# Tokens of the eight late groups turned by 32x32 blocks on VectorE, the blocks placed by the store

## The chip, the core and the metric

The kernel runs on one core of a Trainium2 chip. The engines of the core are TensorE (PE in the profile, with PEld for its weight loads), VectorE (DVE), ScalarE (ACT), GpSimd (POOL) and SyncE (SP, which issues most of the transfers). The metric is the device time of one execution in microseconds. Shown with the time before are three executions; their median is 906.98 us.

## The reference

Two blocks follow each other. The first is a linear attention with decay over 4 batches, 8 heads, 768 tokens and 64 features a head. The second takes its output as 4 x 768 tokens of 512 features and does a Fourier mix, a normalisation and a two-layer MLP:

```python
X = np.fft.fft(x, axis=1)
X = np.fft.fft(X, axis=2)
u = x + np.real(X).astype(np.float32)
mu = np.mean(u, axis=-1, keepdims=True)
var = np.mean((u - mu) ** 2, axis=-1, keepdims=True)
un = (u - mu) / np.sqrt(var + 1e-06)
ch = np.maximum(un @ w_ch1, 0.0) @ w_ch2
return (u + ch).astype(np.float32)
```

Here w_ch1 is 512 x 2048, w_ch2 is 2048 x 512, and all values are float32.

## The kernel before

Each batch goes through `attn` (six chunks of 128 tokens, `attn_chunk`) and then through `fft_ln`. In `fft_ln` the tokens and features are folded on VectorE, five products with a table give the transform along the sequence (L440, copied to `ys`), and then three passes (t = 1, 2, 0) do the transform along the features: `width` makes five products (L453 to L458) into a PSUM tile `ps`, ScalarE copies parts of it to `bs` and `ds`, and VectorE adds the result to two token tiles of 128 x 512, `u` and `v_` (L509 to L513). These two tiles are a pair, and the pair is a group (b, g) of 256 tokens. Behind t = 0 a single row is handled apart (L519 to L522).

`norm(g)` takes the pair: statistics per token (L470, L471), the inverse deviation `rs` on GpSimd (L474, L475), and for each of the two tiles the normalised tokens `un` on VectorE (L482, two halves of 256 features, the second one reversed). The MLP needs features on the partitions, so TensorE transposes `un` in four 128 x 128 pieces into PSUM (L486), and ScalarE copies them into `ut` (L487). `un` has one buffer.

There are twelve groups, in the order (1, 2, 0) for each batch. The first four (`PLAIN`, all of batch 0 and group 1 of batch 1) keep `ut` on the chip and go through `mlp`: 64 products with w1 (L545, relu by ScalarE and VectorE into `hr`), then 32 with w2 (L559), then `y` (L565, L566) and a store. The last eight (`LATE`: groups 2 and 0 of batch 1, and all of batches 2 and 3) store `ut` to device memory as `utd` (L494), 512 KB a group, and the tokens as `ud` (L497). They are read back when attention and Fourier mix are through: `load_u` (L611) loads two groups as `ur`, and `late(j)` does the MLP of both at once by sums and differences of blocks (L627 and L674 are its products). `combine_weights` prepares the sums of weight blocks for it on VectorE (L604), and L617 to L620 those of the tokens.

Program order comes from `weave`, which mixes generators by estimated durations: batches 1 to 3 are the leading work, and the early groups' `mlp` is drawn in between so that TensorE has something to do. The framework then orders the instructions of each engine anew when the kernel is built, so what stands in a queue is read from the compiled order. Within an engine's queue instructions start in that order, and one that waits holds up all behind it. This holds for SP too: the loads of `k`, `q` and `v` for attention, the stores of `utd` and `ud`, and the loads of `ur` share its queue.

## Time and profile before

| What | Value |
|---|---|
| median of three executions | 906.98 us (904.29 to 907.66) |
| the profiled execution: time, span | 908.43 us, 906.4 us |
| granted TensorE clock, mean of that execution | 0.975 |
| attention of batch 0, weights loaded and rebuilt | up to about 115 us |
| other batches, early groups' MLP in between | up to 513 us |
| late groups' MLP | 513 us to the end |
| transposes at L486 | 96 (24 tiles of four), 118 to 491 us |
| copies at L487 | 24, 13.6 us of ScalarE |
| stores of `utd` | 8, 512 KB each, 3.3 us to landing |

The span is what the trace covers; the time also holds what lies around it. Rows of the trace give the start in microseconds, the duration, engine, line, and output from inputs; in square brackets the engine's idle time just before and what ended it. Rows of the chain that ended last give start, duration, engine, output and line. Rows of waits give who waited for whom, the total, how often, and the longest. Rows of stretches give the stretch and its length, busy time and count for PE, PEld, DVE, ACT and POOL, then granted clock, DMA share and GB/s. Rows of transfers give count, KB each, and median microseconds from issue to landing.

### The profile page before, as it was taken

To read this page: it belongs to the slowest core of one execution; us is meant where nothing else is said; L and a number is where in the kernel's file an instruction comes from. 1 tells how busy PE (TensorE), PEld (TensorE's weight loads), DVE (VectorE), ACT (ScalarE), POOL (GpSimd) and SP (SyncE) were. 2 spreads that over 40 slices of the span, in tenths; PEclk is the share of its full clock that TensorE was granted. 3 is DMA by queue.
4 is the path that set the end of the run, shared out by engine and by line. 5 is a ranking of instruction groups with operands and counts; after the bars stand their busy time and mean duration, and the time that the engine had idled before them with its cause. 6 is when DMAs were issued, how large, how long until landed. Compare 5 with 4: busy or idle time off the path is not lost.

```text
span 906.4 us, 11761 instructions
## 1 busy us (share of the span) xinstructions
PE 826.5 (91%) x4660; PEld 652.9 (72%) x4660; DVE 437.0 (48%) x1006; ACT 209.0 (23%) x467; POOL 90.7 (10%) x108
## 2 busy tenths in 40 slices
PE   4775678699999999999999899999999999999997
PEld 2564566545865578567874588888888888888886
DVE  4779869854532135443567756115531454135410
ACT  3665436620211212223221021002200120012100
POOL 2214211100010110012200100000000000000000
PEclk9988789899999999999999999999999999999999
DMA  9899316611013241344216001110011100110010
GB/s 230 232 249 252 111 52 179 209 39 35 24 47 93 74 120 47 116 141 129 88 47 215 29 1 47 46 35 12 1 59 47 35 1 1 47 47 1 0 35 24
DMA packets 96190, 72.43 MB, mean 80 GB/s; under 512 B 77536, under 2 KB 79080, under 8 KB 96136
## 3 DMA queue, kind: packets, MB, share of 16 engines
q1 hardware_dynamic: 90176, 57.51, 22.3%
q0 software_dynamic: 2496, 7.87, 2.7%
q10 hardware_dynamic: 3464, 6.30, 2.0%
q8 instruction: 37, 0.61, 0.3%
q14 instruction: 17, 0.14, 0.0%
HBM read 50.68 MB, written 20.99 MB: 79 GB/s over the span
## 4 chain that ended last, share of the span: by engine, by line
PE 51%; DVE 5%; issue 1%; DMA 1%; POOL 1%; ACT 0%; POOLq 0%; DVEq 0%; ACTq 0%
PE p L627 21%; PE p L674 21%; PE pm L545 1%; PE pm L559 1%; PE pa L440 1%; PE pa L486 1%; PE pa L290 1%; PE pa L322 1%; DVE stt L470 1%; DVE w1s L604 1%; DVE w2s L604 1%; PE pa L318 1%; POOL rs L475 0%; DVE x L512 0%; DVE x L513 0%
## 5 line engine op out<-in xcount | busy, mean ns | idle before, releaser
L545 PE MATMUL pm<-ut,w 128*128 128x256 f32 x512 | 124.2, 392 | 10.0 <-ACT hr L553 8.2
L559 PE MATMUL pm<-w,hr 128*128 128x512 f32 x256 | 120.6, 602 | 0.0
L545 PEld LDWEIGHTS pm<-ut,w 128*128 128x128 f32 x512 | 95.9, 194 | 26.3 <-ACT hr L553 8.9
L627 PE MATMUL p<-ur,w 128*128 128x256 f32 x384 | 95.1, 382 | 3.3 <-DVE ur L620 1.9
L627 PEld LDWEIGHTS p<-ur,w 128*128 128x128 f32 x384 | 73.3, 191 | 14.5 <-issue 2.3
L559 PEld LDWEIGHTS pm<-w,hr 128*128 128x128 f32 x256 | 44.8, 190 | 40.3 <-issue 38.8
L627 PE MATMUL p<-us,w1s 128*128 128x256 f32 x256 | 66.6, 383 | 0.0
L674 PE MATMUL p<-w,hs 128*128 128x256 f32 x256 | 58.0, 379 | 0.5 <-DVE y L695 0.5
L674 PE MATMUL p<-w2s,hs 128*128 128x256 f32 x256 | 57.9, 379 | 0.0
L674 PE MATMUL p<-w,ha 128*128 128x256 f32 x256 | 57.9, 379 | 0.0
L535 POOL DMA_INDIRECT out_dram<-y,ix x12 | 13.3, 1109 | 409.9 <-DVE y L698 370.9
L627 PEld LDWEIGHTS p<-us,w1s 128*128 128x128 f32 x256 | 49.2, 192 | 6.9
L674 PEld LDWEIGHTS p<-w,hs 128*128 128x128 f32 x256 | 48.5, 190 | 7.5 <-DVE y L695 0.9
L674 PEld LDWEIGHTS p<-w2s,hs 128*128 128x128 f32 x256 | 48.6, 190 | 6.6
L674 PEld LDWEIGHTS p<-w,ha 128*128 128x128 f32 x256 | 48.6, 190 | 6.6
L290 PEld LDWEIGHTS pa<-qT,kT 64*128 64x128 f32 x384 | 30.1, 193 | 25.9 <-ACT qT L279 14.4
L654 ACT COPY ha<-p 128x256 f32<-128x256 f32 x32 | 11.9, 372 | 155.6 <-PE p L627 155.5
L290 PE MATMUL pa<-qT,kT 64*128 64x128 f32 x384 | 36.2, 291 | 11.7 <-ACT qT L279 10.0
L294 DVE TENSOR_TENSOR sc<-pa,decay 128x512 f32<-128x512 f32 x48 | 31.8, 684 | 29.1 <-PE pa L290 26.3
L322 PE MATMUL pa<-sc,v 128*64 128x128 f32 x384 | 31.2, 290 | 9.8 <-DVE sc L294 9.8
L665 DVE TENSOR_TENSOR ha<-p,ha 128x256 f32<-128x256 f32 x32 | 13.6, 425 | 47.1 <-ACT ha L664 47.1
L322 PEld LDWEIGHTS pa<-sc,v 128*64 128x64 f32 x384 | 23.4, 143 | 17.5 <-DVE sc L294 13.4
(141 smaller groups left out, 1188.3 us busy)
## 6 DMA issues: line engine op xcount, KB each, us to landing
raw<-in_moe_w_ch_dram SPq DMA_DIRECT2D x32, 512.0 KB, 5.2
k<-in_k_dram SPq DMA_DIRECT2D x24, 256.0 KB, 3.8
q<-in_q_dram SPq DMA_DIRECT2D x24, 256.0 KB, 3.9
v<-in_v_dram SPq DMA_DIRECT2D x24, 256.0 KB, 3.2
ud<-x SPq DMA_DIRECT2D x16, 256.0 KB, 2.1
utd<-ut SPq DMA_DIRECT2D x8, 512.0 KB, 3.3
u<-ud SPq DMA_DIRECT2D x16, 256.0 KB, 2.6
ur<-utd SPq DMA_DIRECT2D x8, 512.0 KB, 5.6
```

Of the source, the lines that this page charges most:

```text
L290: mm(pss[hi][:, hp, :], lhsT=kT[HD[hi], hp, :], rhs=qT[HD[hi], hp, :], start=True, stop=True)
L294: nc.vector.tensor_tensor(t, pss[hi], decay[:, hi::2, :], op=ALU.mult)
L318: mm(po[HD[hi], hp, :], lhsT=s_old[HD[hi], hp, :], rhs=qs[HD[hi], hp, :], start=(hp == 0), stop=False, skip_group_check=True)
L322: mm(po[HD[hi], hp, :], lhsT=vt[:, 2 * hp + hi, :], rhs=sc[hi][:, hp, :], start=(c == 0 and hp == 0), stop=(hp == HP - 1), skip_group_chec ...
L535: nc.gpsimd.indirect_dma_start(out=out.rearrange("b s d -> (b s) d"), out_offset=row_of(2 + HC * (b + 1) + T - HC), in_=y[:, :], in_offset ...
L545: nc.tensor.matmul(ps, lhsT=w1[:, c, 128 * fc:128 * fc + 128], rhs=ut[:, c, :], start=(c == 0), stop=(c == KO - 1))
L559: nc.tensor.matmul(ps, lhsT=hr[fc // 4][:, fc % 4, 128 * i:128 * i + 128], rhs=w2[:, fc, :], start=(fc == 0), stop=(fc == FO - 1))
L604: V.tensor_tensor(o[:, i:i + n // 2], x[:, i:i + n // 2], y[:, i:i + n // 2], op=op)
L627: nc.tensor.matmul(ps, lhsT=s2.A[a][:, kt, 128 * i:128 * i + 128], rhs=U[b][:, kt, :], start=(first and kt == 0), stop=(kt == 1), skip_gro ...
L654: nc.scalar.copy(a11, two(X))
L665: V.tensor_tensor(a22, two(Z), a22, op=ADD)
L674: nc.tensor.matmul(ps, lhsT=h[a][:, s, i, :], rhs=s2.B[b][:, i, :], start=(first and i == 0), stop=(i == HF - 1), skip_group_check=True)
```

## The change

For the eight late groups, `un` is no longer transposed by TensorE. VectorE transposes each 32 x 32 block of `un` in place of its own position (one instruction for a 128 x 512 tile) into a new tile `uq`, which has one buffer. That leaves 16 blocks of features for each of four bands of 32 tokens on the wrong partitions. Four stores for each tile, one for each band of 32 partitions, put the blocks where `utd` has them, in runs of 32 values (128 bytes). The PSUM tile, the copy to `ut` and the one store of `ut` for each group are gone for these groups. The four early groups stay as they were. From this place on, lines of the new kernel are numbered ten higher at the most (L486 is L492, L611 is L621, and so on).

```diff
-            ut = new(up, [128, KO, G * 128], "ut")
+            plain = (b, g) in PLAIN
+            if plain:
+                ut = uts[b, g] = new(up, [128, KO, G * 128], "ut")
+            else:
+                to = utd[b, g] = dram.tile([128, KO, G * 128], F32, name=f"utd{b}{g}")
             for i in range(G):
...
-                pt = psum_a([128, KO, 128])
-                for c in range(KO):
-                    nc.tensor.transpose(pt[:, c, :], un[:, 128 * c:128 * c + 128], ident)
-                nc.scalar.copy(ut[:, :, 128 * i:128 * i + 128], pt)
+                if plain:
+                    pt = psum_a([128, KO, 128])
+                    for c in range(KO):
+                        nc.tensor.transpose(pt[:, c, :], un[:, 128 * c:128 * c + 128], ident)
+                    nc.scalar.copy(ut[:, :, 128 * i:128 * i + 128], pt)
+                else:
+                    uq = new(np_, [128, DM], "uq", bufs=1)
+                    nc.vector.transpose(uq, un)
+                    for r in range(0, 128, 32):
+                        dst = to[:, :, 128 * i + r:128 * i + r + 32].rearrange("(a d) c n -> d c a n", d=32)
+                        src = uq[r:r + 32].rearrange("p (c a n) -> p c a n", c=KO, n=32)
+                        nc.sync.dma_start(dst, src)
                 yield 0.7
-            if (b, g) in PLAIN:
-                uts[b, g] = ut
+            if plain:
                 return
-            utd[b, g] = dram.tile([128, KO, G * 128], F32, name=f"utd{b}{g}")
-            nc.sync.dma_start(utd[b, g], ut)
             for T in TT[g]:
```

## The prediction

> **What bounds the kernel now.** I read the page's engine table first, then the granted clock and busy time by stage, then the chain that ended last.
>
> ```profile
> PE 826.5 (91%) x4660; PEld 652.9 (72%) x4660; DVE 437.0 (48%) x1006; ACT 209.0 (23%) x467; POOL 90.7 (10%) x108
> 225.00:513.00 288.00, 276.37 (x1693) 192.21 (x1692) 134.52 (x288) 59.52 (x147) 37.07 (x48) 0.99 0.30 91
> 513.00:906.00 393.00, 387.15 (x1784) 339.87 (x1784) 142.81 (x390) 47.69 (x127) 7.68 (x8) 1.00 0.08 26
> ```
>
> From 225 us on TensorE (PE) is busy 96% of the time at a granted clock of 0.99 or 1.00, VectorE (DVE) less than half. The later stage, from 513 us, has no instruction that the change touches. So the question lies between 225 and 513 us: how much PE work and PE idleness goes there, and what replaces it. The chain at one of the eight late groups (batch 2, group 1) reads: start, duration, engine, output, line.
>
> ```profile
> 371.49 0.60 DVE x L513
> 372.10 1.20 DVE stt L470 x2
> 373.91 0.74 POOL rs L475
> 374.67 0.42 DVE un L482
> 375.14 0.76 PE pa L486 x4
> 375.90 0.86 PE pm L559 x2
> 376.76 0.44 PE pa L486 x4
> 378.09 0.24 PE pa L458 x2
> ```
>
> The transposes (L486) stand in PE's queue ahead of the next pair's width products (L453 to L458, ending at 378.33), so PE and the chain both pass through normalisation before the next pair starts. The end of the stage:
>
> ```profile
> 507.69 1.03 PE L627 MATMUL p<-ur,w 128*128 128x256 f32 x4
> 510.16 1.10 PE L627 MATMUL p<-ur,w 128*128 128x256 f32 x4 [1.45 <-DVE y L566]
> 513.14 1.22 PE L627 MATMUL p<-ur,w 128*128 128x256 f32 x2 [1.87 <-DVE ur L620]
> ...
> 505.62 0.33 DVE y L566
> 505.95 2.11 DVE w L604 x2
> ...
> 509.28 0.41 DVE y L565
> 509.69 0.33 DVE y L566
> 510.02 1.13 DVE w L604
> 511.15 0.61 DVE us L617
> 512.48 0.61 DVE ur L620
> ```
>
> Here PE has finished the early groups' products and waits 1.45 + 1.87 = 3.3 us for DVE, which is still combining weights.
>
> **The change, part by part.** It removes 16 sets of four transposes and their 16 ScalarE copies, adds 16 DVE block transposes, and replaces 8 stores by 64.
>
> *Transposes.* A set that follows other work takes 0.44 us (the row at 376.76): 16 x 0.44 = **7.0 us** of PE, all in a stretch where PE is 96% busy. PE also waits for `un` ahead of the first set of a group:
>
> ```profile
> PE pa L486 <- DVE un L482: 4.4, 8, 0.8
> 237.95 0.67 PE L486 MATMUL pa<-ident,un 128*128 128x128 f32 x4 [0.67 <-DVE un L482]
> ```
>
> Of these 4.4 us (225 to 516 us), 0.67 belong to an early group that stays. So **3.7 us** of waiting go too. The ScalarE copies cost nothing now, since no PE wait in that view names `ut`; I count them at nothing in both directions, and without them PSUM buffers only come free sooner.
>
> *What is late next.* The compiled order changes more than the diff. Before, on PE, in batch 2 (`pm` from `w`,`hr` are early-group products used as filler; `pa` from `dt`,`ys` are width products):
>
> ```order
> L486 MATMUL pa_2666<-ident,un_2663 128x128 x4
> L559 MATMUL pm_3205<-w_148,hr_2904 128x512
> L486 MATMUL pa_2675<-ident,un_2672 128x128 x4
> L453 MATMUL pa_2687<-dt,ys_151 128x128
> L454 MATMUL pa_2687<-dt,ys_149 128x129
> ```
>
> After, at the same place on PE:
>
> ```order
> L458 MATMUL pa_2629<-dt,ys_152 128x128
> L453 MATMUL pa_2681<-dt,ys_151 128x128
> L454 MATMUL pa_2681<-dt,ys_149 128x129
> L455 MATMUL pa_2681<-dt,ys_153 128x129
> L456 MATMUL pa_2681<-dt,ys_150 128x128
> L458 MATMUL pa_2681<-dt,ys_152 128x128
> L453 MATMUL pa_2741<-dt,ys_151 128x128
> ```
>
> The three pairs' width products now run back to back, and the next batch's first attention chunk follows at once. Its score products `sc` stand on DVE behind the normalisation of the first two pairs. The costs of the filler and of a chunk, from the chain:
>
> ```profile
> 405.85 1.09 PE pa L290 x16
> ...
> 411.96 1.72 PE pm L559 x4
> 413.68 1.09 PE pa L290 x16
> 414.77 0.61 PE pa L305 x16
> ...
> 419.37 0.44 PE pa L277 x4
> 419.80 1.73 PE pm L545 x8
> ```
>
> An L545 product (two instructions) costs 1.73 / 4 = 0.43 us, an L559 product 0.86 us; a chunk takes 413.68 - 405.85 = 7.8 us. Until the first use of `sc`, PE has width products 1.13 (377.20 to 378.33) twice, 0.7 for the single row, 0.88 for two chunk transposes, 2 + 9 L545 products (4.7), 1.09 and 0.61: about 10.2 us. DVE has, from the same starting point, 0.6 us until its inputs are there, six 128x256 pieces for `ds` (6 x 0.33), four 128x512 pieces for `x` (2.4), two pairs of statistics (2 x 1.2), 0.2, the wait for `rs` less what fills it (374.67 - 373.30 - 0.67 = 0.7), two `un` (2 x 0.67), one block transpose and one `sc` (1.2): about 10.8. PE waits some 0.6 us there and as much for the second `sc`; I take 2 us each time with hand-overs, at two batch changes: **+4 us**.
>
> *The block transpose.* The trace has none. From below, 0.33 us, a 128x256 piece; from above 1.13 us, a 128x1024 piece (the row at 510.02). I take 0.6, the 128x512 piece at 371.49, its own size and type: 16 x 0.6 = 9.6 us of DVE, which is idle half of this stretch. At 1.13 the two batch changes would lose about 0.5 us each; at 0.33 they would gain 0.3.
>
> *The stores, and the wait they add.* `uq` has one buffer, so a block transpose waits until all four stores of the tile before have landed, and DVE's in-order queue waits with it. I call the time from the end of a block transpose to that moment L.
>
> ```profile
> v<-in_v_dram SPq DMA_DIRECT2D x24, 256.0 KB, 3.2
> ud<-x SPq DMA_DIRECT2D x16, 256.0 KB, 2.1
> 371.52 0.92 SPq L497 DMA_DIRECT2D ud<-x  x2
> q1 hardware_dynamic: 11477, 2.97, 32.8%
> ```
>
> The last row is the queue between 400 and 440 us, mostly 256-byte packets: 0.328 x 16 x 40 us / 11477 = 18 ns of an engine each. A tile now goes out as 4 x 512 = 2048 packets of 128 bytes, 128 for each of 16 engines, 2.3 us at 18 ns. The fourth issue comes 3 x 0.6 = 1.8 us after the first (0.92 - 0.32 between two). From below, L = 1.8 + 2.1 = 3.9 us (the fourth store lands like a `ud` store); from above, two `v` loads one after the other, also 2048 packets, 6.4 us. I take **5 us**, between the two and nearer to the packets' own sum (0.2 + 2.1 + 2.3 = 4.6).
>
> Does anything wait 5 us? In attention, one block transpose stands in each chunk:
>
> ```order
> L310 TENSOR_TENSOR st_143<-st_143,pa_2946 128x256
> L497 STREAM_TRANSPOSE uq_2714<-un_2711 128x512
> L487 TENSOR_SCALAR un_2720<-x_2444,mv_2699,rs_2707 128x256 x2
> L561 TENSOR_SCALAR hr_2996<-pm_3022 128x256
> L282 TENSOR_TENSOR qs_3020<-pa_3013,qpow 128x512
> L294 TENSOR_TENSOR sc_3038<-pa_3028,decay 128x512
> L294 TENSOR_TENSOR sc_3040<-pa_3029,decay 128x512
> L310 TENSOR_TENSOR st_142<-st_142,pa_3048 128x256
> L497 STREAM_TRANSPOSE uq_2723<-un_2720 128x512
> ```
>
> That is DVE in batch 3's second and third chunk. Behind each wait stand `hr`, `qs` and `sc`, and PE waits for those. A chunk took 7.8 us; by the compiled order batch 3's second to fifth chunks now carry more filler (6, 14 and 12 L545, then 4 and 8 L559 products) and should take some 8 to 13 us, so L up to 7 hides everywhere, and up to about 10 in most. On SP's queue the four stores have moved in between loads:
>
> ```order
> L261 DMA k_3100<-in_k_dram 128x8x64
> L501 DMA utd_2710<-uq_2714 128x4x32 x4
> L261 DMA q_3101<-in_q_dram 128x8x64
> L261 DMA v_3102<-in_v_dram 128x8x64
> L501 DMA utd_2710<-uq_2723 128x4x32 x4
> L261 DMA k_3200<-in_k_dram 128x8x64
> ```
>
> So the next chunk's `q` is issued only after a block transpose and four issues (2.4 us); it has the rest of a chunk, above 5 us, to land in about 4. Cost nothing while that cover lasts. The packets add 2048 x 18 ns / 16 = 2.3 us of all engines to a 7.8 us chunk, whose queue share was 0.33.
>
> *The tail.* After batch 3's first width products, PE now has 56 L545 and 32 L559 products left by the compiled order, against 17 and 32 before: 56 x 0.43 + 32 x 0.86 + width products 2.5 = 54 us. DVE's way to `us` is shorter, about 39 us, since the pairs no longer wait for PE: ds, x and statistics of three pairs 9.8 us, the single row 0.7, ten halves of `un` 3.4, four block transposes 2.4, eight `hr` 2.6, fourteen weight pieces 15.8, one wait for `rs` 1.2, `us` 2.4. So the 3.3 us at the end go, unless the last block transposes are late: they stand ahead of the last `y`, whose PSUM buffer PE's third late product needs. Five waits follow each other: 6.5 + 5 x (L + 0.6) against 54 gives L = 8.9 us, with 5 us lost per us beyond. **-3.3 us.**
>
> Sum: -7.0 - 3.7 - 3.3 + 4.0 = **-10.0 us**. The profiled execution has a span of 906.4 and a time of 908.43 us, so 898.4; the median, 906.98, lies 1.45 us (0.16%) below it, and I forecast from the median: **897 us**.
>
> The Trainium skill, page "DMA: Bandwidth & Descriptors", section Specifications, speaks against the change: below 512 B a transfer misses line rate, because the DMA engine reads, modifies and writes. This trace has only loads of such small packets (18 ns each), no store, so no run so far shows it. By the rule a packet might cost twice as much, L would be 0.2 + 2.1 + 4.6 = 6.9 us, and by the bounds above the sum would hardly move; by the loads' rows it stays as it is.
>
> **The rivals.** *PE finds other waits* (same, about 905). The filler that stood beside each pair is spent elsewhere, and `sc` or a late `q` stops PE some 1 us in eight chunks: -10 + 8. For it: the compiled order is wholly rearranged. Against: PE had 100% busy stretches with as little filler (the chunk at 419.37). *DVE takes PE's place on the path* (same, 903): the work leaves PE, but at 1.13 us a block transpose, and with ScalarE's copies for `ds` late, DVE sets the two batch changes, 3 us more each, -10 + 6. For it: PE and DVE came out within 1 us of each other there. Against: the 512-element rows of one operand all lie near 0.6. *Small stores are slow* (slower). If a stored packet costs more than twice a loaded one, L passes 8.9 us and the five waits of the tail decide: at L = 12 the tail loses 15.5 us and four chunks of batch 3 some 2 us each beyond their own length, -10 + 24 = 921. It breaks even at L = 10.5. For it: the rows show no small store. Against: even twice 4.6 is 9.2.
>
> **How the numbers follow.** Forecast, 891 to 903: 0.70. PE's other waits 0.13, block transposes on the path 0.05, slow stores 0.12 (of it 0.02 near no change). A measurement of this kernel can tell about 0.5%, 4.5 us, from no change. Faster 0.71, same 0.18, slower 0.11. The range, 889 to 908, takes in the forecast and most of the two middle cases; leaving out the slow stores leaves out no more than 0.2.
>
> **What would show it.** Right: no PE work at the removed line from 246 us on, except early groups; late products start without a wait for `y` or `ur`; block transposes near 0.6 us; landings of `utd` stores under 6 us; DVE waiting for its own stores in total under 5 us. Wrong: waits of block transposes on store landings of several us each, `sc` or `qs` becoming PE's releasers, block transposes above 1.1 us, or `k` and `q` loads landing later than about 4 us.

## The result, and the profile after

The changed kernel took 884.63 us (median of four executions, 881.96 to 885.68) against 907.32 us (904.29 to 909.7) for the kernel before on the same chip: a ratio of 0.9747, with a 95% interval of 0.971 to 0.9785. That is 22.7 us, where the prediction had 10. The profiled execution has a time of 881.96 us and a span of 879.7 us, at a mean granted clock of 0.982 (0.975 before).

The page's engine row and the busy time by stage of the changed kernel (stretch, its length, then PE, PEld, DVE, ACT, POOL, and granted clock, DMA share, GB/s):

```profile
PE 805.3 (92%) x4596; PEld 640.9 (73%) x4596; DVE 443.9 (50%) x1022; ACT 199.1 (23%) x451; POOL 91.0 (10%) x108
225.00:491.00 266.00, 260.15 (x1636) 184.48 (x1636) 141.31 (x302) 50.59 (x132) 36.13 (x48) 1.00 0.40 100
491.00:879.00 388.00, 382.56 (x1772) 336.63 (x1770) 141.32 (x387) 47.23 (x126) 7.67 (x8) 1.00 0.08 26
```

PE is busy for 21.2 us less (826.5 before), and only 64 of its instructions are gone. Sixteen sets of transposes at 0.44 us are 7.0 us, so most of the 21.2 us must come from work that the diff does not touch. The groups of PE instructions between 225 and 516 us show which. Before:

```profile
L559 PE MATMUL pm<-w,hr 128*128 128x512 f32 x192 | 92.6, 605 | 0.0
L545 PE MATMUL pm<-ut,w 128*128 128x256 f32 x355 | 85.0, 387 | 0.0
L290 PE MATMUL pa<-qT,kT 64*128 64x128 f32 x192 | 20.8, 285 | 1.7 <-DVE sc L294 1.7
L486 PE MATMUL pa<-ident,un 128*128 128x128 f32 x72 | 11.6, 282 | 4.4 <-DVE un L482 4.4
```

After (L559, L545 and L486 are now L569, L555 and L492):

```profile
L569 PE MATMUL pm<-w,hr 128*128 128x512 f32 x192 | 86.8, 597 | 0.0
L555 PE MATMUL pm<-ut,w 128*128 128x256 f32 x354 | 83.9, 385 | 0.5 <-ACT hr L563 0.5
L290 PE MATMUL pa<-qT,kT 64*128 64x128 f32 x192 | 14.1, 285 | 0.0
L492 PE MATMUL pa<-ident,un 128*128 128x128 f32 x8 | 1.3, 282 | 0.7 <-DVE un L487 0.7
```

As many score products (L290) as before are busy for 6.7 us less, and as many down products of the early groups (L559, now L569) for 5.8 us less. The time of one instruction has hardly moved (285 ns, 605 to 597 ns); what changed is how they lie beside each other. One attention chunk of batch 2 shows it, first before:

```profile
263.78 1.16 PE L290 MATMUL pa<-qT,kT 64*128 64x128 f32 x8
264.87 1.13 PE L559 MATMUL pm<-w,hr 128*128 128x512 f32 x2
265.92 1.16 PE L290 MATMUL pa<-qT,kT 64*128 64x128 f32 x8
267.01 1.12 PE L559 MATMUL pm<-w,hr 128*128 128x512 f32 x2
```

and then after:

```profile
257.18 1.16 PE L290 MATMUL pa<-qT,kT 64*128 64x128 f32 x16
```

The 16 score instructions of a chunk belong to two halves, `hi` = 0 and 1, whose operands lie on partitions 0 to 63 and 64 to 127. In program order the halves take turns, and 16 instructions take 1.16 us. In the six chunks of batch 2 before, the compiled order had sorted them by half, with early-group work between; then 8 instructions take the same 1.16 us, and a chunk costs 1.09 us more. The filler between them costs more too: 1.05 us a product from 264.87 to the next start at 265.92. In a long run it costs 0.86 us, and also 0.86 between two sets of transposes (the prediction's row at 375.90), so the extra 0.19 us shows only beside attention products. After the change all chunks stand in turns, and the early groups' work stands in fewer, longer pieces: 65 pieces by the compiled order, 93 before. I call a chunk of the first kind **sorted** below, and the early groups' products between other work **filler**.

To add it up I count each piece of PE work from its start to the start of the next, less the idle time, from batch 1's first width product to the first product of the late groups (**stage**), and from there to the start of the last run of 16 products (**late part**). The stage begins at these two rows, before and after:

```profile
230.38 0.38 PE L453 MATMUL pa<-dt,ys 128*128 128x128 f32 x2
```

```profile
228.84 0.38 PE L453 MATMUL pa<-dt,ys 128*128 128x128 f32 x2
```

and ends at 507.69 before, at 486.04 after (below). It is 277.3 us long before and 257.2 us after:

| Part | Before | After | Difference |
|---|---|---|---|
| transposes' own time | 8.6 | 0.9 | -7.7 |
| PE waiting for `un` | 4.4 | 0.7 | -3.7 |
| score products | 19.6 | 13.3 | -6.3 |
| filler | 168.9 | 164.9 | -4.0 |
| other idle time of PE | 3.8 | 5.1 | +1.3 |
| everything else, by difference | 72.0 | 72.3 | +0.3 |
| stage | 277.3 | 257.2 | -20.1 |
| late part | 389.5 | 384.4 | -5.1 |

What lies ahead of the stage is 1.5 us shorter, but the change touches none of its work, and over all the profiles below it ends between 225 and 237 us. Where a few us matter I therefore compare stage and late part and not spans.

One difference in this table lies in the clock. In the kernel before, PE's granted clock is 0.50 in two stretches of 3.4 us, each right behind waits of PE. The first begins at 338.9 us, the second at 512.9 us, behind the waits of 1.45 and 1.87 us that the prediction quotes. The first wait and the work behind it, and two windows inside the stretches, before:

```profile
337.65 1.16 PE L290 MATMUL pa<-qT,kT 64*128 64x128 f32 x8 [1.70 <-DVE sc L294]
338.74 2.85 PE L545 MATMUL pm<-ut,w 128*128 128x256 f32 x6
339.00:342.00 3.00, 3.00 (x11) 1.99 (x12) 2.33 (x5) 0.39 (x1) 0.00 (x0) 0.50 0.00 0
513.00:516.00 3.00, 2.86 (x7) 2.31 (x8) 1.31 (x4) 0.00 (x0) 0.00 (x0) 0.50 0.23 87
```

Three L545 products take 2.8 us there instead of 1.3. I call what PE's work loses in such stretches **half clock**: half of the time that the work takes in them. It is 1.7 us in the stage (1.3 us of it in the filler) and 1.6 us in the late part before, and nothing in either after the change. In every trace of this case each such stretch between the start of the stage and the last product lasts 3.4 us or a multiple of it, and begins right behind 3.4 us in which PE had been idle for 1.7 us or more. So a wait of PE can cost more than its own length.

The end of the stage after the change, PE and then VectorE (start, duration, engine, line, output from inputs):

```profile
464.58 21.62 PE L569 MATMUL pm<-w,hr 128*128 128x512 f32 x50
486.04 6.52 PE L637 MATMUL p<-ur,w 128*128 128x256 f32 x28
```

```profile
471.52 0.68 DVE L629 TENSOR_TENSOR us<-ur,us 128x512 f32<-128x512 f32 x1
...
480.52 0.70 DVE L497 STREAM_TRANSPOSE uq<-un 128x512 f32<-128x512 f32 x1
486.24 0.42 DVE L575 TENSOR_TENSOR y<-pm,x 128x256 f32<-128x256 f32 x1 [5.02 <-PE pm L569]
```

The late products start without a wait. `us` is done at 472.2 us, 13.8 us ahead of need, and DVE waits for PE. All waits of PE from 225 to 500 us (who for whom, total, times, longest):

```profile
PE pa L440 <- DVE fe L409: 2.0, 2, 1.3
PE pa L322 <- DVE sc L294: 0.9, 1, 0.9
PE pa L305 <- issue: 0.8, 1, 0.8
PE pa L329 <- ACT oT L325: 0.7, 1, 0.7
PE pa L492 <- DVE un L487: 0.7, 1, 0.7
PE pm L555 <- ACT hr L563: 0.5, 1, 0.5
PE pa L440 <- DVE fe L405: 0.2, 1, 0.2
```

The block transposes and their stores, and four issues on SP's queue:

```profile
L501 SPq DMA_DIRECT2D utd<-uq x64: 570/622/1740, 247.0 to 483.5; - x64
L497 DVE STREAM_TRANSPOSE uq<-un x16: 689/703/712, 246.2 to 480.5; 128x512 f32<-128x512 f32 x16
its engine sat idle before it (us, times) until:
who waited for it (us, times):
...
DMA to landing us min/median/max: 2.2/2.2/3.5
```

```profile
340.55 2.87 SPq L501 DMA_DIRECT2D utd<-uq  x4
```

A block transpose takes 0.70 us, a store lands 2.2 us after its issue in the median, and both lists are empty: DVE never sat idle ahead of a block transpose, so none stood in its queue for the stores of the one before.

### The profile page after: what moved, and what is told of

The parts are those of the page before. It is cut to its first block, busy times and chain, and to the rows that moved or that the text cites. A ratio compares the mean times of both kernels' runs of the same rounds, so it can differ in the third digit from the quotient of the medians.

```text
span 879.7 us, 11692 instructions
## 1 busy us (share of the span) xinstructions
PE 805.3 (92%) x4596; PEld 640.9 (73%) x4596; DVE 443.9 (50%) x1022; ACT 199.1 (23%) x451; POOL 91.0 (10%) x108
## 4 chain that ended last, share of the span: by engine, by line
PE 71%; DVE 8%; issue 6%; DMA 4%; POOL 1%; ACT 1%; POOLq 0%; DVEq 0%; ACTq 0%
PE p L637 22%; PE p L684 22%; PE pm L555 8%; PE pm L569 8%; PE pa L440 3%; DMA raw<-in_moe_w_ch_dram 3%; PE pa L322 2%; PE pa L290 1%; DMA x<-xb,ix 1%; PE pa L318 1%; DVE pw L235 1%; PE pa L305 1%; PE pa L329 1%; PE pa L272 1%; PE pa L277 1%
## 5 line engine op out<-in xcount | busy, mean ns | idle before, releaser
L555 PE MATMUL pm<-ut,w 128*128 128x256 f32 x512 | 123.1, 389 | 10.9 <-ACT hr L563 9.2
L555 PEld LDWEIGHTS pm<-ut,w 128*128 128x128 f32 x512 | 95.0, 193 | 28.0 <-ACT hr L563 10.2
L569 PE MATMUL pm<-w,hr 128*128 128x512 f32 x256 | 114.9, 597 | 0.0
L569 PEld LDWEIGHTS pm<-w,hr 128*128 128x128 f32 x256 | 47.1, 190 | 51.7 <-issue 51.1
L545 POOL DMA_INDIRECT out_dram<-y,ix x12 | 11.8, 982 | 428.9 <-DVE y L708 368.4
L684 PEld LDWEIGHTS p<-w,hs 128*128 128x128 f32 x256 | 48.6, 190 | 7.4 <-DVE y L705 0.9
L664 ACT COPY ha<-p 128x256 f32<-128x256 f32 x32 | 11.9, 372 | 172.8 <-PE p L637 172.8
L322 PE MATMUL pa<-sc,v 128*64 128x128 f32 x384 | 33.1, 298 | 11.3 <-DVE sc L294 11.3
L282 DVE TENSOR_TENSOR qs<-pa,qpow 128x512 f32<-128x512 f32 x20 | 13.8, 689 | 51.6 <-ACT qT L279 51.5
L290 PE MATMUL pa<-qT,kT 64*128 64x128 f32 x384 | 29.4, 291 | 9.8 <-ACT qT L279 9.8
L290 PEld LDWEIGHTS pa<-qT,kT 64*128 64x128 f32 x384 | 24.5, 193 | 18.9 <-ACT qT L279 15.5
```

The lines of the kernel that those rows point to most:

```text
L282: nc.vector.tensor_tensor(qs, ptq, qpow, op=ALU.mult)
L290: mm(pss[hi][:, hp, :], lhsT=kT[HD[hi], hp, :], rhs=qT[HD[hi], hp, :], start=True, stop=True)
L322: mm(po[HD[hi], hp, :], lhsT=vt[:, 2 * hp + hi, :], rhs=sc[hi][:, hp, :], start=(c == 0 and hp == 0), stop=(hp == HP - 1), skip_group_chec ...
L545: nc.gpsimd.indirect_dma_start(out=out.rearrange("b s d -> (b s) d"), out_offset=row_of(2 + HC * (b + 1) + T - HC), in_=y[:, :], in_offset ...
L555: nc.tensor.matmul(ps, lhsT=w1[:, c, 128 * fc:128 * fc + 128], rhs=ut[:, c, :], start=(c == 0), stop=(c == KO - 1))
L569: nc.tensor.matmul(ps, lhsT=hr[fc // 4][:, fc % 4, 128 * i:128 * i + 128], rhs=w2[:, fc, :], start=(fc == 0), stop=(fc == FO - 1))
```

## The experiments

Two explanations of the missing 12.7 us stood at first. **Theory A**: a good part of the gain comes from the order in which the unchanged products came out (score halves in turns, filler in fewer pieces). **Theory B**: all of it comes from the transposes and the waits at them, and the rest is coincidence of one profile. From e6 on, **A2** is A with a second part: how much filler the order leaves for the time after batch 3's first width product decides whether PE has to wait for VectorE at the end. Ratios are to the kernel before on the same chip, with 95% intervals. The columns "left", "pieces" and "sorted" are read from the compiled orders (filler left at batch 3's first width product, at 0.43 us for an L545 product and 0.86 us for an L559 product; pieces of filler; sorted chunks), the others from the traces. "Waits" is PE's idle time in stage and late part together, "half clock" what its work lost there at the clock of 0.50, and "work" the rest of the two.

| Kernel | Sorted | Pieces | Left, us | Stage, us | Late part, us | Waits, us | Half clock, us | Work, us | Ratio |
|---|---|---|---|---|---|---|---|---|---|
| before | 6 | 93 | 34.8 | 277.3 | 389.5 | 12.1 | 3.3 | 651.4 | 1 |
| changed | 0 | 65 | 51.6 | 257.2 | 384.4 | 6.3 | 0 | 635.3 | 0.9747 |
| e1 | 0 | 65 | 5.2 | 285.2 | 404.0 | 37.3 | 8.2 | 643.7 | 1.0195 |
| e2 | 6 | 63 | 51.6 | 260.3 | 384.4 | 6.9 | 0 | 637.9 | 0.9726 |
| e3 | 0 | 64 | 51.6 | 264.3 | 384.1 | 10.2 | 3.1 | 635.1 | 0.9752 |
| e4 | 6 | 91 | 11.2 | 294.2 | 404.2 | 38.6 | 6.9 | 653.0 | 1.0323 |
| e5, changed again | 0 | 65 | 51.6 | 257.4 | 384.4 | 6.5 | 0 | 635.4 | 0.9735 |
| e6 | 0 | 45 | 51.6 | 329.7 | 384.1 | 55.3 | 16.1 | 642.3 | 1.0545 |
| e7 | 0 | 73 | 13.8 | 261.3 | 408.8 | 30.5 | 5.9 | 633.6 | 1.0069 |
| e8 | 0 | 73 | 32.7 | 255.8 | 397.5 | 13.1 | 4.6 | 635.6 | 0.9863 |
| e9 | 0 | 37 | 68.8 | 344.9 | 384.1 | 64.0 | 23.3 | 641.7 | 1.062 |
| e10 | 1 | 58 | 34.0 | 262.7 | 385.2 | 8.8 | 1.7 | 637.4 | 0.9762 |
| e11 | 0 | 58 | 68.8 | 283.6 | 384.1 | 23.4 | 9.5 | 634.7 | 1.0023 |
| e12 | 0 | 51 | 87.7 | 291.5 | 384.1 | 29.5 | 11.9 | 634.2 | 1.0092 |
| e13 | 1 | 61 | 36.5 | 272.2 | 384.4 | 10.2 | 1.7 | 644.7 | 0.9889 |
| e14 | 6 | 88 | 48.6 | 275.0 | 384.4 | 8.9 | 0 | 650.6 | 0.9936 |
| e15 | 0 | 75 | 51.6 | 263.7 | 384.1 | 6.5 | 0 | 641.4 | 0.9783 |
| e16 | 0 | 61 | 58.5 | 261.5 | 384.1 | 9.2 | 0 | 636.4 | 0.9797 |
| e17, changed again | 0 | 65 | 51.6 | 257.5 | 384.4 | 6.6 | 0 | 635.3 | 0.972 |

### e1: the kernel before, score products kept in program order

```diff
-                mm(pss[hi][:, hp, :], lhsT=kT[HD[hi], hp, :], rhs=qT[HD[hi], hp, :], start=True, stop=True)
+                i = mm(pss[hi][:, hp, :], lhsT=kT[HD[hi], hp, :], rhs=qT[HD[hi], hp, :], start=True, stop=True)
+                if hp + hi:
+                    tc.keep_in_program_order(i)
```

> The kernel before, with one thing fixed: the eight score products of a chunk (L290) stay in program order, the two head halves in turn; transposes and stores as before. In the compiled order no chunk of batch 2 has its score products sorted by half any more (6 had), and the early groups' products stand in 65 pieces among the other work, as in the changed kernel, against 93. Theory A, that about 10 us of the gain are the compiled order (6.3 us score products, 4.0 us filler pieces): about 897 us, 10 below before, up to 13 if the wait at the start of the late groups goes too. Theory B, that all of the gain comes from the transposes' own work and what waits for it: 907 us, no change.

Measured: 928.37 us, ratio 1.0195 (1.0134 to 1.0256). Both theories missed. The cheaper work is there: score products and filler take PE 10.1 us less than in the kernel before (1.3 us of it half clock). But the order that came out had used up its filler: 5.2 us of it were left at batch 3's first width product, and the transposes were still on PE. The waits of PE that grew, from 200 us on:

```profile
PE pa L488 <- DVE un L484: 16.3, 11, 5.8
PE p L629 <- DVE us L620: 15.1, 1, 15.1
```

Behind these waits the clock was 0.50 for a while, which cost another 8.2 us (3.3 before). So cheap products alone gain nothing, and theory A as it stood was not enough.

### e2: the changed kernel, score products of batch 2 sorted by half

```diff
-        for hp in range(HP):
-            for hi in range(2):
-                mm(pss[hi][:, hp, :], lhsT=kT[HD[hi], hp, :], rhs=qT[HD[hi], hp, :], start=True, stop=True)
+        for hp, hi in ([(p, i) for i in range(2) for p in range(HP)] if b == 2 else
+                       [(p, i) for p in range(HP) for i in range(2)]):
+            i = mm(pss[hi][:, hp, :], lhsT=kT[HD[hi], hp, :], rhs=qT[HD[hi], hp, :], start=True, stop=True)
+            if b == 2 and hp + hi:
+                tc.keep_in_program_order(i)
```

> The changed kernel, with the score products of batch 2's six chunks sorted by head half, as the kernel before had them; 63 pieces of filler, as in the changed kernel (65). Theory A: 6 x 1.09 = 6.5 us more than the changed kernel, about 891 us, and L290 about 20 us instead of 13 between 225 us and the late groups. Theory B: 885 us.

Measured: 887.56 us, ratio 0.9726 (0.967 to 0.9781). By time this says nothing, since the interval holds both expectations. By the stage it is 3.1 us longer, and the score products of that batch take 9.8 us instead of 6.7 us: half of what sorting had cost before. There filler stood between the halves, here it does not, so a sorted chunk costs its full 1.09 us only when the halves are also pulled apart.

### e3: the changed kernel, one plain store for each tile

```diff
-                    for r in range(0, 128, 32):
-                        dst = to[:, :, 128 * i + r:128 * i + r + 32].rearrange("(a d) c n -> d c a n", d=32)
-                        src = uq[r:r + 32].rearrange("p (c a n) -> p c a n", c=KO, n=32)
-                        nc.sync.dma_start(dst, src)
+                    nc.sync.dma_start(to.rearrange("p c n -> p (c n)")[:, DM * i:DM * i + DM], uq)
```

> The changed kernel with the block transpose kept, but each tile stored by one transfer of 2 KB rows instead of four of 128-byte runs (the blocks are not placed, so the late groups get other numbers). If the small packets and the four issues are hidden, as forecast: 884 us, within 1. If they cost: 875 to 880.

Measured: 890.43 us, ratio 0.9752 (0.9694 to 0.9811). The blocks are left where they lie, so a tile goes out in rows of 2 KB in one store instead of 2048 packets of 128 bytes in four. It is no faster; its stage is 7.1 us longer: PE's waits are 3.9 us longer (5.0 us for `sc`, 0.9 us in the changed kernel; why stays open), and 3.1 us are half clock. Its work is the changed kernel's within 0.2 us. Nothing here shows that the small stores cost the changed kernel any time.

### e4: the changed kernel, with the PE transposes of `un` done too

```diff
+                ut2 = new(up, [128, KO, G * 128], "ut")
...
                     nc.vector.transpose(uq, un)
+                    pt = psum_a([128, KO, 128])
+                    for c in range(KO):
+                        nc.tensor.transpose(pt[:, c, :], un[:, 128 * c:128 * c + 128], ident)
+                    nc.scalar.copy(ut2[:, :, 128 * i:128 * i + 128], pt)
```

> The changed kernel, with TensorE's transposes and ScalarE's copies of the late groups done as well (their result is not used). The compiled order goes back to 6 chunks with sorted score products and 91 pieces of filler. Theory A: 884.6 + 7.7 (transposes) + 10.3 (order) + 2 to 5 (waits) = 905 to 908 us. Theory B, the transposes' work and its waits alone: 895 us.

Measured: 940.22 us, ratio 1.0323 (1.0264 to 1.0382). Both missed again. As theory A has it, the six sorted chunks and 91 pieces came back with the transposes. But only 11.2 us of filler were left for the end, and PE waited there as in e1: 15.6 us for `un` in front of the transposes and 16.9 us for `us`.

### e5: the changed kernel again, as a control

> The changed kernel once more, as the reference for the three beside it: ratio to before 0.975 by all theories.

Measured: 883.59 us, ratio 0.9735 (0.9671 to 0.98), as in the first measurement (0.9747).

### e6 and e9: the transposes kept, and filler held back by hand

e6 is e1 with the products of the last early group kept behind all that is traced ahead of them:

```diff
+    HELD = PLAIN[3:]
...
+                if c == 0 and (b, g) in HELD:
+                    tc.keep_in_program_order(i)
...
+                if fc % 4 == 0 and (b, g) in HELD:
+                    tc.keep_in_program_order(m)
```

> The kernel before with its transposes, copies and stores; score products in program order as in e1, and the last early group's products held behind what is traced ahead of them, so that 56 w1 and 32 w2 products (51.6 us) are left at batch 3's first width product, as in the changed kernel (before: 34.8 us, e1: 5.2). Theory A2, that the order gives its 10.7 us and that what is left at that point decides the wait ahead of the late groups: 12 to 17 us below before (ratio 0.981 to 0.987), and the remaining 8 to 10 to the changed kernel are the transposes. Theory B, that the transposes' work and its waits make the whole gain: ratio 0.995 to 1.00.

e9 also holds half of the third group's down products, and traces filler later:

```diff
+    H1, H2 = {PLAIN[j]: n for j, n in ((3, 0),)}, {PLAIN[j]: n for j, n in ((2, 16),)}
...
+                if c == 0 and fc >= H1.get((b, g), 99):
+                    tc.keep_in_program_order(i)
...
+                if fc % 4 == 0 and i * 16 + fc >= H2.get((b, g), 999):
+                    tc.keep_in_program_order(m)
...
-    run(weave(fr, back, (len(PLAIN) * t_mlp - FO * 1.7 - 25.0) / t_rest))
+    run(weave(fr, back, (len(PLAIN) * t_mlp - FO * 1.7 - 45.0) / t_rest))
```

> The kernel before with its PE transposes kept, the score products in program order (head halves in turn everywhere), the last early group's products and the second token tile of the third group's width... of its down products held behind what is traced ahead, and the weave's number 45: 37 pieces of early-group products instead of 93, 82.6 us of them left at batch 2's first width product (82.6 before) and 51.6 at batch 3's (34.8 before, 51.6 after). Theory A2 (transposes 8 us, cheaper products 10.7, and a cover of products for the last batch): the order is had without the change, so score products -6.3, pieces 56 fewer at 0.15 us (-8), end wait -3, less some waits of PE for un that the held products no longer cover (+0 to +8): 892 to 900, ratio 0.981 to 0.992. Theory B (PE's transposes and the waits in front of them are all of it): no gain, 0.995 to 1.005. Rival C (with the transposes on PE any order that saves products pays in waits for un, as in e6): 1.00 to 1.03.

Measured: e6 955.57 us, ratio 1.0545 (1.048 to 1.061); e9 967.77 us, ratio 1.062 (1.0577 to 1.0662). Both far outside what A2 and B expected; only the direction of e9's rival C held, not its size. The end of the stage is covered now (late part 384.1 us in both), but filler is missing earlier. In e9's trace 68.8 us of filler are left at batch 2's first width product as well as at batch 3's, not the 82.6 and 51.6 us of the expectation: between 358 and 488 us none runs at all. The waits of PE in e9 between 225 and 580 us:

```profile
PE pa L488 <- DVE un L484: 27.3, 14, 5.9
PE pa L442 <- DVE fe L411: 23.2, 2, 12.4
```

With the transposes of `un` in PE's queue, one that finds too little filler ahead of it waits for VectorE, 5.9 us at the longest. Work fell by 9.1 us in e6 and 9.7 us in e9 against the kernel before, as the order should make it; but the waits grew by 43 and 52 us, and half clock by 13 and 20 us. These two kernels do not measure the transposes by themselves; they show how much filler the waits at them want.

### e7, e8, e16 and e11, e12: where the filler stands

The number 25 in the weave sets how early filler is drawn in beside batches 1 to 3. Nothing else is changed in e7 (-15), e8 (5) and e16 (45):

```diff
-    run(weave(fr, back, (len(PLAIN) * t_mlp - FO * 1.7 - 25.0) / t_rest))
+    run(weave(fr, back, (len(PLAIN) * t_mlp - FO * 1.7 - (5.0)) / t_rest))
```

> The changed kernel with one number of the weave changed (25 to -15), so that the early groups' products come earlier and only 16 w2 products (13.8 us) are left at batch 3's first width product, where VectorE has some 42 us to go. Theory A2: 13.8 + 4.2 us of width products against 42, so TensorE waits about 24 us at the end of the stage: 24 us above the changed kernel (ratio about 1.00). Theory B: no change to the changed kernel.

> The changed kernel with the same number at 5: 12 w1 and 32 w2 products, 32.7 us, are left there. Theory A2: 32.7 + 4.2 against 42, about 5 us above the changed kernel (ratio 0.980). Theory B: no change to it.

> The changed kernel with the weave's number 45 instead of 25 and nothing held: 61 pieces (65), 58.5 us of early-group products left at batch 3's first width product (51.6), 103.6 at batch 2's, as in the changed kernel. e7 and e8 had less left there and lost 13 to 30 us, e11 and e12 more and lost 25 to 33 us, so the changed kernel lies in a trough; 58.5 is 7 us to the one side of it. If the trough is wide enough: 882 to 886, ratio 0.971 to 0.976, same as the control. If batch 3's attention already runs short of products: 890 to 898, 0.98 to 0.99.

e11 and e12 (numbers 45 and 65) also hold the third and fourth early group as e6 does the fourth:

```diff
+    HELD = PLAIN[2:]
...
-    run(weave(fr, back, (len(PLAIN) * t_mlp - FO * 1.7 - 25.0) / t_rest))
+    run(weave(fr, back, (len(PLAIN) * t_mlp - FO * 1.7 - 65.0) / t_rest))
```

> The changed kernel with the third and fourth early group's products held behind what is traced ahead, and the weave's number 45 instead of 25: 58 pieces (65), 68.8 us of early products left at batch 3's first width product (51.6), 110.1 at batch 2's (103.6). A2: 7 pieces fewer give -1 us, and the end has cover to spare: 882 to 885, ratio 0.971 to 0.975 beside 0.973 of the changed kernel. If more cover at the end is worth something yet: 0.965 to 0.970. If the attention of batch 3 runs short of early products: 0.975 to 0.99.

> The same with the number 65: 51 pieces, 87.7 us left at batch 3's first width product. A2: 14 pieces fewer give -2 us: 881 to 884, ratio 0.969 to 0.974. If the attention of batch 3 runs short of early products: 0.975 to 1.0, and more than e11.

Measured: e7 913.99 us, 1.0069 (1.0032 to 1.0107); e8 897.69 us, 0.9863 (0.9789 to 0.9936); e16 890.02 us, 0.9797 (0.9771 to 0.9823), on a chip where the changed kernel had 881.71 us; e11 910.23 us, 1.0023 (0.9998 to 1.0048); e12 917.99 us, 1.0092 (1.0059 to 1.0125). A2's direction held in e7 and e8, with losses larger than it had (30 and 14 us, expected 24 and 5); it failed in e11 and e12, where I had expected a small gain and starving was the other case written down. Each of the five shifts from 51.6 us loses. What the table shows of the loss is nearly all waits and half clock: the work stays within 1.7 us of the changed kernel's. Too early, the waits stand at the end (e7, 450 to 540 us; for "issue" the profile names no releaser):

```profile
PE p L637 <- issue: 14.8, 1, 14.8
PE p L637 <- DMA ur<-utd: 8.2, 1, 8.2
PE p L637 <- ACT ha L664: 3.5, 1, 3.5
```

Held back, they stand in the middle, in the Fourier mix of batch 2 and the attention of batch 3 (e11, 225 to 515 us, the two largest):

```profile
PE pa L440 <- DVE fe L405: 8.1, 3, 6.7
PE pa L322 <- DVE sc L294: 7.5, 2, 5.1
```

The cover that the end needs can be read off. In the changed kernel VectorE goes from batch 3's first width product (430.1 us) to `us` (472.2) in 42 us. PE has width products of 4.2 us and the filler that is left: 55.9 us with 51.6 us of it, and no wait. In e8 these are 36.9 us, 5 us short, and PE waits 8.0 us at the late products; in e7 some 18 us, 24 us short, and the waits are the 26.5 us above. In e10 (below), where VectorE has no block transposes to do, 38.2 us of cover leave a wait of only 0.5 us. e16, with 58.5 us of filler left, has more cover than is needed; its stage is 4.0 us longer than that of the changed kernel on its chip (e17), and the rest of its 8 us lies ahead of the stage, where any two profiles differ by some us.

### e10: the transposes left out, the stores as before

```diff
-                pt = psum_a([128, KO, 128])
-                for c in range(KO):
-                    nc.tensor.transpose(pt[:, c, :], un[:, 128 * c:128 * c + 128], ident)
-                nc.scalar.copy(ut[:, :, 128 * i:128 * i + 128], pt)
+                if (b, g) in PLAIN:
...
+                else:
+                    nc.scalar.copy(ut[:, :, 128 * i:128 * i + 128], un.rearrange("p (c n) -> p c n", c=KO))
```

> Leaves out the transposes of the eight later groups altogether: ACT copies un into ut untransposed, and the 512 KB store of ut stays as before; no block transpose, no small stores. Compiled order: 1 of the chunks of batch 2 sorted by half, 58 pieces, 34.0 us of early products left at batch 3's first width product (before 34.8, after 51.6). Theory A2: transposes -7.8, score products -5.5, pieces -4, waits for un -2.4; the end wait stays as before or grows as in e8 (+0 to +13): 888 to 900, ratio 0.979 to 0.992. If the block transpose and its stores were themselves what gains (ACT's copies gone, ut's store earlier), little gain: 0.99 to 1.00. If they cost anything worth telling, this kernel is faster than the changed one: below 0.97.

Measured: 887.55 us, ratio 0.9762 (0.9725 to 0.9798), just under what A2 expected (0.979 to 0.992). This kernel has no block transpose and no small store, and it gains what the changed kernel gains. So the 22.7 us come from what left PE and from how its queue came out, and VectorE's 11.2 us of block transposes and the 64 stores neither add to the gain nor take from it by more than the intervals, some 4 us, can tell.

### e13, e14 and e15: PE transposes that wait for nothing

All three do the 16 sets of four PE transposes, but of the identity tile, which is there from the start. e13 is e10 with these transposes, read by nobody; in e14 ScalarE copies their PSUM tile to `ut`, as before the change; e15 is the changed kernel with them.

```diff
 e13
+                    pt = psum_a([128, KO, 128])
+                    for c in range(KO):
+                        nc.tensor.transpose(pt[:, c, :], ident, ident)
                     nc.scalar.copy(ut[:, :, 128 * i:128 * i + 128], un.rearrange("p (c n) -> p c n", c=KO))
 e14
-                    nc.scalar.copy(ut[:, :, 128 * i:128 * i + 128], un.rearrange("p (c n) -> p c n", c=KO))
+                    pt = psum_a([128, KO, 128])
+                    for c in range(KO):
+                        nc.tensor.transpose(pt[:, c, :], ident, ident)
+                    nc.scalar.copy(ut[:, :, 128 * i:128 * i + 128], pt)
 e15
                     nc.vector.transpose(uq, un)
+                    pt = psum_a([128, KO, 128])
+                    for c in range(KO):
+                        nc.tensor.transpose(pt[:, c, :], ident, ident)
```

> The kernel of e10 (ACT copies un to ut untransposed) with the 16 sets of four PE transposes of the eight later groups put back, but of the identity tile, which is there from the start, and read by nobody: PE's time of the transposes without any wait for un. The compiled order is nearly e10's: 1 chunk sorted, 61 pieces (58), 36.5 us of early products left at batch 3's first width product (34.0). If PE's own time counts in full: e10's 887.6 + 7.7 = 893 to 897, ratio 0.983 to 0.988. If it hides in PE's idle time: 887 to 889, ratio 0.975 to 0.979. If the order, not the transposes, is all of e10's gain: 0.976 too.

> As the one with unread transposes, but ACT copies their PSUM tile to ut, as before the change, so that the PSUM tile is held until ACT has read it. The compiled order turns into that of before: 6 chunks sorted by head half, 88 pieces (before 93), 48.6 us of early products left at batch 3's first width product. PE's own transposes are the same as in the unread kernel, and none waits for un. Theory A2: sorted chunks and 27 more pieces make it 8 us slower than the unread kernel: 900 to 906, ratio 0.990 to 0.996. Rival B (the wait for un and the transposes' own time are all of the gain): the same as the unread kernel within 2 us.

> The changed kernel with four PE transposes of the identity tile beside each block transpose, read by nobody: 0 chunks sorted, 75 pieces (65), 103.6 and 51.6 us left, as in the changed kernel. PE's own time alone: +7.7 us and 10 pieces at 0.15 us: 891 to 894 beside 884.6, ratio 0.981 to 0.985. If this time hides: 0.974 to 0.976.

Measured: e13 898.89 us, ratio 0.9889 (0.9837 to 0.9941); e14 902.47 us, 0.9936 (0.9908 to 0.9964); e15 888.39 us, 0.9783 (0.9738 to 0.9827).

e15 puts the transposes' own time back into an order with the same filler left and no sorted chunk. It costs 6.2 us of stage and late part together against the first profile of the changed kernel (5.9 us against e17's), and 0.36% or 3.3 us by the ratios, whose intervals overlap. e13 against e10 shows the same time in the other kernel: 8.7 us by stage and late part, 11.5 us by the ratios. The transposes' own time, 7.2 and 7.1 us in the traces of e13 and e15 when counted as above, lies between the two values by stage and late part.

e13 and e14 have the same PE instructions in these stages, and none of the late groups' transposes waits for `un`. They differ in what ScalarE copies: in e14 the PSUM tile, which is held until it is read, in e13 `un`, whose one buffer is held until then. Which of the two turns the order was not tried. With e14's copy the order of the kernel before comes back, six sorted chunks and 88 pieces. The groups of PE instructions, 225 to 516 us, e13:

```profile
L565 PE MATMUL pm<-w,hr 128*128 128x512 f32 x192 | 87.6, 602 | 0.0
L290 PE MATMUL pa<-qT,kT 64*128 64x128 f32 x192 | 15.7, 285 | 0.6 <-ACT qT L279 0.6
```

and e14:

```profile
L565 PE MATMUL pm<-w,hr 128*128 128x512 f32 x192 | 93.1, 607 | 0.0
L290 PE MATMUL pa<-qT,kT 64*128 64x128 f32 x192 | 20.8, 285 | 2.9 <-DVE sc L294 2.9
```

These are the rows of before and after the change once more (92.6 and 20.8, 86.8 and 14.1), now without any difference in the transposes. The work that this order saves is 5.9 us (650.6 against 644.7). In time it is worth less than theory A2's 8 us: 2.8 us of stage, since e13 waits 1.3 us more and loses 1.7 us at half clock, and 3.6 us by the medians, with overlapping intervals. So the times alone do not exclude rival B, the same time within 2 us; the rows show cheaper products, which B does not have.

### e17: the changed kernel on e16's chip

> The changed kernel, unchanged, on the same chip as e16: 0.9735 to 0.9747 by the two earlier measurements.

Measured: 881.71 us, ratio 0.972 (0.9696 to 0.9743). No kernel tried here was shown to be faster than the changed one.

## Why the prediction was right in direction and too small

**The transposes' own time, -7.0 us: right.** The trace has 7.7 us less, e15 and e13 put 6 to 9 us back by stage and late part.

**PE's waits for `un`, -3.7 us: right.** 4.4 us before, 0.7 us after, which belong to the early group, as predicted.

**The wait at the end, -3.3 us: right, by its own reason, but a wait was priced at its own length alone.** The prediction set 54 us of PE work against 39 us of VectorE's way to `us` (its terms add up to 38.3); the trace has 55.9 against 42. The late part is 5.1 us shorter: 3.3 us of waits, and 1.6 us of half clock that had followed them. With the 1.7 us of half clock in the stage that is 3.3 us that the prediction put at nothing. Its own quoted rows had a sign of it: at 510.16 four instructions take 1.10 us, at 513.14, behind the second wait, two take 1.22 us. e14 has the same late part as the changed kernel with the PE transposes still there, but with 48.6 us of filler left and no wait for `un`. It gained 7.4 us over the kernel before by stage and late part, 5.8 us by the medians. That this is close to 3.7 + 3.3 = 7.0 is luck: the waits at `un` and at the end are 7.0 us shorter there, but other waits are 3.9 us longer, and 3.3 us of half clock went.

**New waits at the batch changes, +4.0 us: mis-sized.** The race between PE and VectorE was worked out as 10.2 against 10.8 us, and then 2 us were taken for each change with hand-overs. The trace has one wait for `sc` of 0.9 us, and PE's idle time outside `un` grew by 1.3 us in the stage.

**The step that failed: "What is late next. The compiled order changes more than the diff."** It read the new order only for waits, and let every product that the diff does not touch keep its time. In the trace those products are 10.3 us cheaper (score products 6.3, filler 4.0), 9.0 us without the half clock in the filler. The rows for it stood in the trace of before: eight score instructions of one half at 263.78, as long as 16 at 405.85, which the prediction quotes. It took the price of a chunk from batch 3, where the halves were in turns already, and never looked at batch 2, where they were sorted. With this term and half clock the sum is -7.0 - 3.7 - 3.3 + 1.3 - 9.0 - 3.3 = -25.0 us. Stage and late part of the two profiled executions differ by 25.2 us; the medians are 22.7 us apart, less than these two executions.

How firmly is that term shown? That the products are cheaper, and that the order makes them so, is shown by three pairs (before and after, before and e1, e14 and e13). The column "work" gives the size with waits and half clock taken out. From the kernel before to e1, e6 and e9, which keep the transposes but have no sorted chunk and fewer pieces, work falls by 7.7, 9.1 and 9.7 us; from e14 to e13 by 5.9 us, with one sorted chunk left. The transposes' part is 6.1 us (e15 against the changed kernel) and 7.3 us (e13 against e10). Before and after the change the difference is 16.1 us in all. So I put the order at 6 to 10 us of PE's work; the waits and half clock that went make up the other 9.1 us between the two profiles.

What the order is worth in time is less sure, since waits move with it. In e1, e6 and e9 more than all of it was lost to waits and half clock, and between e14 and e13 the 5.9 us give 2.8 us. From e10 to the changed kernel stage and late part fall by another 6.3 us (2.1 us of work, 2.5 us of waits, 1.7 us of half clock), but the ratios there differ by 1.4 us only (of 908), within their intervals. The finer division of the 22.7 us stays open.

**The rivals.** *Small stores are slow* fell: four issues take 2.87 us, a store lands 2.2 us after its issue, and nobody waited; from the end of the block transpose at 340.5 us to the last landing it is 4.5 us, near the 5 us predicted. What a small packet costs a DMA engine shows in the queue's row between 480 and 487 us of the changed kernel, where the last tile's four stores go out:

```profile
q1 hardware_dynamic: 2112, 0.26, 24.3%
```

That is 0.243 x 16 x 7 us / 2112 = 13 ns of an engine each, less than the 18 ns of the 256-byte loads that the prediction used, so the packet at twice that price, its estimate from the Trainium skill's rule (page "DMA: Bandwidth & Descriptors", section Specifications), does not show here. By the byte the small packets are dear all the same. The queue over the whole execution, the changed kernel and then e3, which stores the same bytes in 2 KB rows:

```profile
q1 hardware_dynamic: 122816, 57.51, 25.4%
```

```profile
q1 hardware_dynamic: 91328, 57.51, 23.1%
```

e3 needs (0.254 x 879.7 - 0.231 x 888.5) x 16 = 291 us of engine time less, of 32768 x 13 ns = 426 us, or 27 us on all sixteen engines. The waits of PE and DVE shown above name none of these stores. *DVE takes PE's place* fell too: the block transposes took 0.70 us in their rows, 11.2 us in all, as long as the addition that the prediction priced at 0.6 us from the chain (0.68 us in its row), and `uq` made nobody wait. *PE finds other waits* came to 1.3 us and not 8. But it named the right place: e7, e8, e11 and e12 show that the changed kernel has little to spare there, with 12 to 33 us lost when the same filler stands elsewhere.

## What to carry to other kernels

When an engine is full and a scheduler orders its queue, price the new order as well as the removed work: compare, product by product, how the unchanged instructions lie beside each other before and after, for neighbours that ran together may come apart, and the other way round. Filler has two customers, the waits in the middle and the wait at the end; count how much the order leaves at each before believing that a removed or cheapened instruction is worth its own time. Price a wait of a full PE with the clock behind it: in these traces the stretch after a wait could run at half the clock. A PE instruction that waits for a late VectorE result costs its own time and all the filler that has to stand ahead of it, which is why keeping the transposes while improving the order lost in e1, e6 and e9, and half clock came on top.

## What the runs showed of the hardware

Products with a 64-row contraction on partitions 0 to 63 and 64 to 127 run beside each other when they stand in turns: 16 of them take 1.16 us, as long as 8 of one half. This agrees with the Trainium skill, page "TensorEngine Tiling (Array Packing)", section Key Properties, by which tiles of the array work independently. A 128x512 product that stands alone between attention products costs 1.05 us from its start to the next, against 0.86 us in a run or between 128x128 transposes. Stretches at a granted clock of 0.50 lasted 3.4 us or a multiple of it, and each began behind 3.4 us in which PE had been idle for 1.7 us or more; they cost PE's work 3.3 us in the kernel before and 23.3 us in e9. Packets of 128 bytes stored to device memory took 13 ns of a DMA engine each, and a 64 KB store of them landed in 2.2 us (2.2 to 3.5). A 32x32 block transpose of a 128x512 float32 tile took 0.70 us on VectorE, about as long as an addition of that size (0.68 us).
